# Rounding a float64 weight tile in one ScalarE pass, one float32 product instead of three, and conv taps on TensorE

## The chip, the cores and the metric

The kernel runs on one core of one Trainium2 chip. The metric is the device time of one execution in microseconds, as the median of several runs; lower is better. Beside it stands one execution that the hardware profiler recorded, and all rows below are from that one.

## The reference

Eight batches pass through three blocks. The weights and the conv taps arrive as float64, all else is float32.

```python
# 1. attention between x (8, 8 heads, 512, 64) and state (8, 8, 32, 64)
xread = softmax(x @ state.T / 8) @ state          # 512 rows per head
sread = softmax(state @ x.T / 8) @ x              # 32 rows per head
x = concat(xread, sread)                          # (8, 544, 512)
# 2. gated block: 5 causal conv taps per channel
gate = sigmoid(sum(conv_w[k] * shift(x, 4 - k) for k in range(5)))
x = (gate * (x @ w_val)) @ w_out                  # moe_w_out, 512 x 512
# 3. second block: 3 centred conv taps per channel
h = relu(x @ w_in)                                # 512 x 1024
gate = sigmoid(sum(conv_w2[k] * shift(h, 1 - k) for k in range(3)))
out = (h * gate) @ w_out2                         # moe2_w_out, 1024 x 512
```

## The kernel before

**Two products in one.** Nothing stands between the first block's output matrix (`w_mid` in the kernel) and the second block's input matrix (`w_in`), so the kernel multiplies the two once, at the start, into `wp` (512 by 1024), and every batch uses `wp`. The same holds for the state rows and `w_val`: `a_sw` multiplies the state by `w_val`, and `a_val` multiplies the attention weights by that.

**Halves.** A float32 tile that TensorE is to multiply is split into a high half `hi` (a ScalarE copy to the type fp32r) and a low half `lo = v - hi` (a subtraction, `low`, L137). A product is then three fp32r matmuls, `three` (L161, L162, L163): hi by hi, hi by lo, lo by hi. Products that are made once, such as the scores (L237) and `vals` (L562), are plain float32 matmuls. In `split`, the letters of the table `HOW` say how a low half leaves PSUM: `_` on VectorE, `a` by a ScalarE copy and a GpSimd subtraction, `p` by a matmul with minus the identity and a ScalarE copy. In the rows of `i0`, `i1` and `o`, `l` puts the subtraction of that tile on VectorE and `_` on GpSimd. `c2` names the tiles of batch 0 whose middle tap is multiplied on VectorE.

**Weights.** `fetch` loads a float64 tile of 128 by 512 as raw words of 512 KB. `to_f32` turns it into float32 by integer work on the two 32-bit words of each element: three ScalarE passes (L151, L152, L153), a shift on VectorE (L156) and an integer addition on GpSimd (L158). There are 24 such tiles: four of `w_mid` (`mid`, tokens `m`), eight of `w_in` (`inp`, tokens `i` and, for the loads of the second half, `j`), four of `w_val` (`val`, tokens `v`), eight of `w_out` (`last`, tokens `l`), and one small tile with all conv taps (`taps`, token `k`).

**Order.** Work is written as generators that are started and advanced in an order that stands in five strings. `LOADS` orders the first DMAs, all of them on SyncE's queue. `ORDER` is the set-up: conversion of `w_mid`, the first half of `w_in` and `w_val`, the first half of `wp` (`product0`, tokens `p`, and its way out of PSUM, tokens `q`) and the attention of batch 0. `AHEAD` holds the 16 half steps in which batch b prepares batch b + 1: `L` and `X` load, `t` prepares the state, `x` transposes x, `s` scores, `e`, `r` and `y` read, `w` is `a_sw`, `V` is `a_val`. `AMONG` adds to the steps of batch 0 the second half of `w_in`, the second half of `wp` (`product1`) and `w_out`. `CLOSING` orders the last batch together with the state rows of all batches. The strings set the order of the program; the tile framework then places the instructions on the engines' queues, and each engine works through its own queue in order.

**Steady work.** Per batch and per each of eight blocks of 128 columns, `z_unit` makes 12 matmuls into `z` and the conv and gate (`conv2` L427, `gate2` L432 to L436), and `o_unit` makes 12 matmuls into `o`, two blocks later.

Of the kernel before, what the change touches and what calls it, by code (L numbers as in the profile page):

```python
# [23 lines left out]

LOADS = """
c m0 m1 m2 m3 i2 j2 a i3 i0 v1 i1 v0 v2 j1 j3 j0 v3
"""
ORDER = """  # L30
m1 m0 k m0 v3 i0 m2 t i0 k m0 m2 i1 k m1 m1 i1 m3 i2 m3 i3 i0 m3 v2 m2 m1 i1 v0 i2 m2 m3 x0 x1 x3
t v1 x2 s s i2 v3 e0 e1 s i3 p0 v1 m0 v2 r0 i3 r0 s y0 p1 y0 p2 v0 w r0 p3 r1 y1 q0 w q2 V0 V0 V1
y0 V1 y1 q1 V2 q3 y1 V3 V2 V3 r1
"""

AHEAD = """
L t x0 | | x1 x2 x3 | s | e0 | w X1 e1 | r0 | y0 | X0 r1 | | y1 | X2 V0 | | | | V2 V1 X3 V3
"""

AMONG = """  # L40
i1 i0 | | l0 i2 i3 | p0 | p3 | l1 | p1 l2 | f p2 | | l4 l3 | | l7 | | l6 l5 | |
"""

CLOSING = """
v1 v2 | v0 | v3 O Z E O Z Z | z1 z0 | | | o0 Z Z | Z z2 z4 O O O z3 | o1 O | Z | | O Z | z6 o2 z5
z7 O O | O | o4 | | o67 o5 o3
"""


HOW = {  # L50
    "i0": "l l l _".split(),
    "i1": "l l l l".split(),
    "o": "_ _ l l l l _ _".split(),
    "mT": "_ _ _ a".split(),
    "w0": "a p _ p".split(),
    "w1": "a _ _ p".split(),
    "sw0": "_ a".split(),
    "sw1": "_ a".split(),
    "c2": "_ d _ _ d _ _ _".split(),
}  # L60


# [1 line left out]
def tile_cross_attention_gated_conv_ffn(  # L64
# [74 lines left out]
    def words(raw, dt, k, of=2):  # L139
        return raw.bitcast(dt).rearrange("p (n k) -> p n k", k=of)[:, :, k]  # L140

    def to_f32(dst, raw):

        hi, lo = words(raw, U32, 1).bitcast(F32), words(raw, U32, 0)  # L150
        nc.scalar.activation(dst, hi, AF.Copy, scale=2.0**-112)  # L151
        nc.scalar.activation(lo.bitcast(I32), lo, AF.Copy, scale=2.0**-29)  # L152
        nc.scalar.activation(words(raw, F16, 1, 4), hi, AF.Copy, scale=2.0**-80)  # L153
        yield 0
        d = dst.bitcast(U32)
        nc.vector.tensor_scalar(d, d, 3, None, ALU.logical_shift_left)  # L156
        d = dst.bitcast(I32)
        nc.gpsimd.tensor_tensor(out=d, in0=d, in1=lo.bitcast(I32), op=ALU.add)  # L158

    def three(ps, wh, wl, mh, ml, first, last):  # L160
        nc.tensor.matmul(ps, wh, mh, start=first, stop=False)  # L161
# [102 lines left out]
    def a_score(b):  # L264
        a = A[b]
        sc = [ps_a.tile([P, S], F32, tag="a", name="sc") for _ in range(NG)]
        by_heads(a, sc, lambda pr, u: a["xT"][pr][u, :])
        parts = [score(a, g, sc[g]) for g in range(NG)]
        next(parts[0])
        yield 1  # L270
        next(parts[1])
        next(parts[0])
        yield 1
        next(parts[1])
        next(parts[0], None)
        yield 1
        next(parts[1], None)

    def score(a, g, sc):
        m2 = att.tile([P, 4], F32, tag="m2", name="m2")  # L280
        nc.vector.reduce_max(m2[:, 0:1], sc, axis=AX.X)
        nc.vector.tensor_scalar_mul(m2[:, 1:2], m2[:, 0:1], -SCALE)
        l1 = s_tile("l1", (P, HB, 32))
        nc.vector.transpose(l1.rearrange("p c j -> p (c j)"), sc)
        e2 = s_tile("e2")
        nc.scalar.activation(e2, sc, AF.Exp, scale=SCALE, bias=m2[:, 1:2], accum_out=m2[:, 2:3])
        a["r2"][g], a["e2", g] = m2, e2
        m1 = att.tile([P, HB, 1], F32, tag="m1", name="m1")
        nc.vector.reduce_max(m1, l1, axis=AX.X)
        e1 = s_tile("e1", (P, HB, 32))  # L290
        nc.gpsimd.tensor_tensor(out=e1, in0=l1, in1=m1.to_broadcast([P, HB, 32]), op=ALU.subtract)
        yield
        nc.scalar.activation(e1, e1, AF.Exp, scale=SCALE)
        nc.vector.tensor_scalar_add(m2[:, 2:3], m2[:, 2:3], EPS)
        nc.vector.reciprocal(m2[:, 3:4], m2[:, 2:3])
        r1 = att.tile([P, HB, 1], F32, tag="r1", name="r1")
        nc.vector.reduce_sum(r1, e1, axis=AX.X)
        nc.vector.tensor_scalar_add(r1, r1, EPS)
        nc.vector.reciprocal(r1, r1)
# [57 lines left out]
    def conv1(t, src, ct, taps):  # L357

        for k in taps:
            nc.vector.scalar_tensor_tensor(  # L360
                out=t, in0=src(k), scalar=cw1(ct, k), in1=t, op0=ALU.mult, op1=ALU.add
            )

    def a_xread(b, g):

        a = A[b]
        ps = [ps_a.tile([P, S], F32, tag="a", name="xr") for _ in range(2)]
        for n, (w, m) in enumerate((("nh", "ah"), ("nh", "al"), ("nl", "ah"))):
# [155 lines left out]
    def product_out(ps, hf, c):
        fs = slice(hf * DM, (hf + 1) * DM)
        run(split(wp[:, 0, c, fs], wp[:, 1, c, fs], ps, HOW[f"w{hf}"][c]))

    def val(k):
        yield from to_f32(wv[:, k, :], RAW["v", k])

    def last(f):
        w = f32_tile(True)
        yield from to_f32(w, RAW["o", f])
        yield 1
        W2[f] = w_tile("w2")
        halves(W2[f], w, nc.vector if "l" in HOW["o"][f] else nc.gpsimd)
# [251 lines left out]
```

## Time and profile before

| | |
|---|---|
| median of 3 runs | 592.46 us (591.95 to 592.55) |
| the profiled execution | 591.2 us, of which the span from the first to the last instruction is 589.4 us |
| mean granted TensorE clock | 0.979 of full speed |
| busy over the span | TensorE 94%, VectorE 72%, ScalarE 64%, GpSimd 50% |

In the rows PE is TensorE, PEld its weight loads, DVE VectorE, ACT ScalarE, POOL GpSimd, and SPq SyncE's DMA queue; L153 is line 153 of the kernel. Durations of neighbouring instructions on an engine overlap by about a tenth of a microsecond, and matmuls overlap by more, so the pitch of a sequence is read from start to start.

### The profile page before, as it was taken

What the parts mean: (1) busy time and instruction counts of PE and PEld (TensorE: products, weight loads), DVE (VectorE), ACT (ScalarE), POOL (GpSimd) and SP (SyncE); (2) the same over time, 40 slices, a digit from 0 to 9 for tenths busy, and PEclk for the clock granted to TensorE, in tenths of its full rate; (3) what the DMA queues carried; (4) which work ended last, traced back from release to release, by engine and by line L of the source; (5) the groups of instructions that cost most, each with busy time, mean ns of one, the idle gap of its engine ahead of it and who ended that gap; (6) DMA issues with size and microseconds to landing.
All of it is one profiled execution on the core that took longest, in us unless ns stands there. A gap on an engine that the chain in (4) does not pass through costs nothing.

```text
span 589.4 us, 8728 instructions
## 1 busy us (share of the span) xinstructions
PE 551.1 (94%) x3036; PEld 410.9 (70%) x3036; DVE 423.2 (72%) x691; ACT 375.8 (64%) x699; POOL 295.4 (50%) x374
## 2 busy tenths in 40 slices
PE   0668799989999999999999999999999999999996
PEld 0344566768677867786778677867786778887884
DVE  1465778888599669966996699579957986753452
ACT  8999867785575557555755575556556656654553
POOL 3375669557364536453646354635363625532431
PEclk9957999989999999999999999999999999999999
DMA  6973301630126012701270126010301000100003
GB/s 227 344 256 51 72 9 33 183 71 2 37 60 128 1 47 54 126 0 61 43 121 2 63 48 115 2 63 19 72 0 54 19 1 2 62 10 0 1 1 108
DMA packets 97933, 37.84 MB, mean 64 GB/s; under 512 B 90422, under 2 KB 90466, under 8 KB 97890
## 3 DMA queue, kind: packets, MB, share of 16 engines
q1 hardware_dynamic: 97890, 37.29, 25.1%
q8 instruction: 24, 0.39, 0.3%
q14 instruction: 19, 0.16, 0.1%
HBM read 28.36 MB, written 8.91 MB: 63 GB/s over the span
## 4 chain that ended last, share of the span: by engine, by line
PE 81%; ACT 12%; POOL 2%; DVE 2%; DMA 1%; issue 1%; ACTq 0%; POOLq 0%
PE o L452 10%; PE z L161 10%; PE o L453 10%; PE o L454 9%; PE z L162 9%; PE z L163 9%; PE sw L237 2%; PE val L161 2%; PE val L162 2%; PE val L163 2%; PE xr L371 2%; ACT wir L153 2%; ACT wor L153 1%; PE sr L322 1%; PE sc L237 1%; PE vals L562 1%
## 5 line engine op out<-in xcount | busy, mean ns | idle before, releaser
L427 DVE SCALAR_TENSOR_TENSOR t<-h,cw,t 128x512 f32<-128x512 f32 x128 | 116.5, 914 | 60.6 <-ACT t L425 59.3
L137 POOL TENSOR_TENSOR f<-t,f 128x512 fp32r<-128x512 f32 x64 | 91.2, 1426 | 31.2 <-ACT f L435 30.1
L452 PE MATMUL o<-w,f 128*128 128x512 f32 x256 | 104.5, 410 | 0.2 <-ACT f L435 0.2
L161 PE MATMUL z<-g,wp 128*128 128x512 f32 x256 | 102.8, 402 | 1.0 <-ACT g L397 0.9
L162 PE MATMUL z<-g,wp 128*128 128x512 f32 x256 | 101.4, 396 | 1.1 <-POOL g L137 1.1
L453 PE MATMUL o<-w,f 128*128 128x512 f32 x256 | 101.3, 396 | 0.0
L163 PE MATMUL z<-g,wp 128*128 128x512 f32 x256 | 101.2, 395 | 0.0
L386 DVE SCALAR_TENSOR_TENSOR t<-xr,cw,t 128x510 f32<-128x510 f32 (+3 forms) x128 | 91.0, 740 | 3.8 <-ACT sT L379 2.8
L432 ACT ACTIVATE t<-t 128x512 f32<-128x512 f32 x64 | 40.6, 634 | 78.4 <-DVE t L427 78.4
L454 PE MATMUL o<-w,f 128*128 128x512 f32 x256 | 78.6, 395 | 0.0
L137 POOL TENSOR_TENSOR g<-v,g 128x512 fp32r<-128x512 f32 (+1 forms) x36 | 47.9, 1329 | 39.3 <-ACT g L397 39.2
L452 PEld LDWEIGHTS o<-w,f 128*128 128x128 f32 x256 | 48.4, 189 | 23.7 <-ACT f L435 6.4
L433 DVE SCALAR_TENSOR_TENSOR t<-t,h 128x512 f32<-128x512 f32 x64 | 52.8, 825 | 14.8 <-ACT t L432 14.1
L161 PEld LDWEIGHTS z<-g,wp 128*128 128x128 f32 x256 | 48.1, 188 | 16.9 <-issue 3.0
L435 ACT ACTIVATE f<-t 128x512 fp32r<-128x512 f32 x64 | 40.5, 633 | 28.3 <-DVE t L433 28.3
L162 PEld LDWEIGHTS z<-g,wp 128*128 128x128 f32 x256 | 48.3, 189 | 12.5 <-POOL g L137 1.9
L163 PEld LDWEIGHTS z<-g,wp 128*128 128x128 f32 x256 | 48.2, 188 | 12.4 <-issue 1.2
L442 POOL MEMSET h<- 128x2 f32 x64 | 6.8, 107 | 97.1 <-DVE t L433 96.6
L453 PEld LDWEIGHTS o<-w,f 128*128 128x128 f32 x256 | 48.6, 190 | 9.3
L454 PEld LDWEIGHTS o<-w,f 128*128 128x128 f32 x256 | 47.1, 188 | 10.1 <-issue 0.4
L443 ACT ACTIVATE h<-z 128x512 f32<-128x512 f32 x64 | 38.5, 601 | 22.1 <-PE z L163 21.2
L425 ACT ACTIVATE t<-h,cw 128x512 f32<-128x512 f32 x62 | 45.3, 731 | 1.6 <-POOL h L442 0.4
(164 smaller groups left out, 1017.4 us busy)
## 6 DMA issues: line engine op xcount, KB each, us to landing
xn<-in_x_dram SPq DMA_DIRECT2D x32, 256.0 KB, 4.1
out_dram<-ob SPq DMA_DIRECT2D x26, 256.0 KB, 2.2
y<-in_x_dram SPq DMA_DIRECT2D x96, 64.0 KB, 2.4
wir<-in_moe_w_in_dram SPq DMA_DIRECT2D x8, 512.0 KB, 7.8
wor<-in_moe_w_out_dram SPq DMA_DIRECT2D x8, 512.0 KB, 7.5
wmr<-in_moe_w_out_dram SPq DMA_DIRECT2D x4, 512.0 KB, 4.2
wvr<-in_moe_w_val_dram SPq DMA_DIRECT2D x4, 512.0 KB, 9.1
out_dram<-ob SPq DMA_DIRECT2D x8, 224.0 KB, 2.3
```

The costliest lines, as they stand in the source:

```text
L137: (e or nc.gpsimd).tensor_tensor(out=out, in0=v, in1=hi.bitcast(F32), op=ALU.subtract)
L161: nc.tensor.matmul(ps, wh, mh, start=first, stop=False)
L162: nc.tensor.matmul(ps, wh, ml, start=False, stop=False)
L163: nc.tensor.matmul(ps, wl, mh, start=False, stop=last)
L386: nc.vector.scalar_tensor_tensor(out=t[:, n:], in0=ps[r][:, 0 : S - n], scalar=cw1(ct, k), in1=t[:, n:], op0=ALU.mult, op1=ALU.add,)
L425: nc.scalar.activation(t, h(1), AF.Copy, scale=cw2(f, 1))
L427: nc.vector.scalar_tensor_tensor(out=t, in0=h(k), scalar=cw2(f, k), in1=t, op0=ALU.mult, op1=ALU.add)
L432: nc.scalar.activation(t, t, AF.Tanh, scale=0.5)
L433: nc.vector.scalar_tensor_tensor(out=t, in0=t, scalar=1.0, in1=h, op0=ALU.add, op1=ALU.mult)
L452: nc.tensor.matmul(ps, ft[:, 0, c], W2[f][:, 0], start=first, stop=False)
L453: nc.tensor.matmul(ps, ft[:, 0, c], W2[f][:, 1], start=False, stop=False)
L454: nc.tensor.matmul(ps, ft[:, 1, c], W2[f][:, 0], start=False, stop=last)
```

## The change

`to_f32` takes a letter. Without it, ScalarE makes one pass: the low word times 2^-51, plus 2.0, written as float32, whose bits are 0x40000000 plus the rounded top bits of the low word. VectorE shifts the high word left by 3 straight from the raw tile, GpSimd adds the two as integers, and a new VectorE step puts the sign bit back. With the letter `s` the three old passes stay, and there is no sign step. `HOW` gives `s` to two of the four `w_mid` tiles, three of the eight `w_in` tiles, one of the four `w_val` tiles and one of the eight `w_out` tiles; so 17 of the 24 tiles and the small tile of taps take the new way.

`w_mid` (transposed) and `w_in` are no longer halved: `mid` makes one copy, `inp` converts into the tile that is multiplied, and `product` is one float32 matmul where it was three fp32r ones. Both now live in tiles of the pool `w` in pairs.

The first conv of batch 0 takes, for its first block of channels, four of five taps by float32 matmuls with diagonal matrices (`taps_by_matmul`). In batches 0 and 1 three small operations of `score` per group move from VectorE to ScalarE. `w0`, `sw1` and `c2` get other letters, and all five order strings are new.

```diff
 LOADS = """
-c m0 m1 m2 m3 i2 j2 a i3 i0 v1 i1 v0 v2 j1 j3 j0 v3
+m3 m0 m1 c m2 i2 a i0 i3 i1 j1 v2 v1 v0 j3 j0 v3 j2
 """
 ORDER = """
-m1 m0 k m0 v3 i0 m2 t i0 k m0 m2 i1 k m1 m1 i1 m3 i2 m3 i3 i0 m3 v2 m2 m1 i1 v0 i2 m2 m3 x0 x1 x3
-t v1 x2 s s i2 v3 e0 e1 s i3 p0 v1 m0 v2 r0 i3 r0 s y0 p1 y0 p2 v0 w r0 p3 r1 y1 q0 w q2 V0 V0 V1
-y0 V1 y1 q1 V2 q3 y1 V3 V2 V3 r1
+i0 m1 i1 m1 m0 t m0 m3 i2 k i3 t i0 i0 k m2 k m2 m1 m0 i2 v2 i1 m3 m3 x3 x0 x1 m2 m2 v3 x2 s e0 v3
+m0 v1 s r0 r0 v1 s i1 e1 i2 y0 p0 m3 v0 v0 v2 m1 w i3 w y0 r0 p1 r1 s y0 i3 p2 V0 p3 r1 V1 V0 y1
+V2 V1 q1 y1 q0 V3 y1 V2 V3 q3 q2
 """
 AHEAD = """
-L t x0 | | x1 x2 x3 | s | e0 | w X1 e1 | r0 | y0 | X0 r1 | | y1 | X2 V0 | | | | V2 V1 X3 V3
+x1 | | L x0 x2 t x3 s | | e0 | | w e1 r0 | y0 | r1 | | X2 y1 X0 V0 | V1 | V3 V2 X1 | | X3 |
 """
 AMONG = """
-i1 i0 | | l0 i2 i3 | p0 | p3 | l1 | p1 l2 | f p2 | | l4 l3 | | l7 | | l6 l5 | |
+i2 l0 i3 i1 l1 | | i0 p0 | l2 p3 | | | f p1 | l4 p2 | l3 | | | l7 | l5 | | | l6
 """
 CLOSING = """
-v1 v2 | v0 | v3 O Z E O Z Z | z1 z0 | | | o0 Z Z | Z z2 z4 O O O z3 | o1 O | Z | | O Z | z6 o2 z5
-z7 O O | O | o4 | | o67 o5 o3
+v1 E v2 v3 | | Z v0 | Z Z z1 | O z0 Z | | o0 Z | Z O O O o1 z2 z4 z3 | | Z | O | | O Z o2 z6 z7 O
+| O | z5 o4 O | o67 | O o5 o3
 """
 HOW = {
-    "i0": "l l l _".split(),
-    "i1": "l l l l".split(),
-    "o": "_ _ l l l l _ _".split(),
-    "mT": "_ _ _ a".split(),
-    "w0": "a p _ p".split(),
+    "m": "_ s s _".split(),
+    "i0": "_ _ s _".split(),
+    "i1": "s s _ _".split(),
+    "v": "_ s _ _".split(),
+    "c1": "t _ _ _".split(),
+    "o": "_ _ l l ls _ _ l".split(),
+    "w0": "p _ _ p".split(),
     "w1": "a _ _ p".split(),
     "sw0": "_ a".split(),
-    "sw1": "_ a".split(),
-    "c2": "_ d _ _ d _ _ _".split(),
+    "sw1": "_ _".split(),
+    "c2": "d d d _ _ d _ d".split(),
 }
...
-        hi, lo = words(raw, U32, 1).bitcast(F32), words(raw, U32, 0)
-        nc.scalar.activation(dst, hi, AF.Copy, scale=2.0**-112)
-        nc.scalar.activation(lo.bitcast(I32), lo, AF.Copy, scale=2.0**-29)
-        nc.scalar.activation(words(raw, F16, 1, 4), hi, AF.Copy, scale=2.0**-80)
+        hi, lo = words(raw, U32, 1), words(raw, U32, 0)
+        d = dst.bitcast(U32)
+        if "s" in how:
+            nc.scalar.activation(dst, hi.bitcast(F32), AF.Copy, scale=2.0**-112)
+            nc.scalar.activation(lo.bitcast(I32), lo, AF.Copy, scale=2.0**-29)
+            nc.scalar.activation(words(raw, F16, 1, 4), hi.bitcast(F32), AF.Copy, scale=2.0**-80)
+        else:
+            nc.scalar.activation(lo.bitcast(F32), lo, AF.Copy, scale=2.0**-51, bias=2.0)
         yield 0
-        d = dst.bitcast(U32)
-        nc.vector.tensor_scalar(d, d, 3, None, ALU.logical_shift_left)
-        d = dst.bitcast(I32)
-        nc.gpsimd.tensor_tensor(out=d, in0=d, in1=lo.bitcast(I32), op=ALU.add)
+        nc.vector.tensor_scalar(d, d if "s" in how else hi, 3, None, ALU.logical_shift_left)
+        nc.gpsimd.tensor_tensor(out=dst.bitcast(I32), in0=dst.bitcast(I32), in1=lo.bitcast(I32), op=ALU.add)
+        if "s" not in how:
+            nc.vector.scalar_tensor_tensor(
+                out=d, in0=hi, scalar=0x80000000, in1=d, op0=ALU.bitwise_and, op1=ALU.bitwise_or
+            )
...
+        def scaled(out, x, by, plus):
+            if early:
+                nc.scalar.activation(out, x, AF.Copy, scale=by, bias=plus)
+            else:
+                nc.vector.tensor_scalar(out, x, by, plus, ALU.mult, ALU.add)
...
-        nc.vector.tensor_scalar_mul(m2[:, 1:2], m2[:, 0:1], -SCALE)
+        scaled(m2[:, 1:2], m2[:, 0:1], -SCALE, 0.0)
...
-        nc.vector.tensor_scalar_add(m2[:, 2:3], m2[:, 2:3], EPS)
+        scaled(m2[:, 2:3], m2[:, 2:3], 1.0, EPS)
...
-        nc.vector.tensor_scalar_add(r1, r1, EPS)
+        scaled(r1, r1, 1.0, EPS)
...
+    def taps_by_matmul(t, ct):
+        diag = s_tile("diag", (P, HALO, P))
+        for k in range(HALO):
+            nc.scalar.activation(diag[:, k], ident, AF.Copy, scale=cw1(ct, k))
+        sums = ps_z.tile([P, S], F32, tag="z", name="taps")
+        nc.vector.memset(sums[:, 0:1], 0.0)
+        for k in range(HALO - 1, -1, -1):
+            n = HALO - k
+            nc.tensor.matmul(
+                sums[:, n:], diag[:, k], t[:, 0 : S - n], start=k == HALO - 1, stop=k == 0, skip_group_check=True
+            )
+        nc.vector.scalar_tensor_tensor(
+            out=t, in0=t, scalar=cw1(ct, HALO), in1=sums, op0=ALU.mult, op1=ALU.add
+        )
...
     def mid(c):
...
-        MT[c] = w_tile("mT")
-        run(split(MT[c][:, 0], MT[c][:, 1], ps, HOW["mT"][c], wm))
+        if (c, "both") not in MT:
+            MT[c, "both"] = MT[c ^ 1, "both"] = w_tile("mT")
+        MT[c] = MT[c, "both"][:, c % 2].bitcast(F32)
+        nc.scalar.activation(MT[c], ps, AF.Copy)
     def inp(hf, k):
-        w = f32_tile(True)
-        yield from to_f32(w, RAW["i", hf, k])
-        yield 1
-        WI[hf, k] = g_tile("wi") if hf else f_tile("wi")
-        halves(WI[hf, k], w, nc.vector if "l" in HOW[f"i{hf}"][k] else nc.gpsimd)
+        if (hf, k, "both") not in WI:
+            WI[hf, k, "both"] = WI[hf, k ^ 1, "both"] = w_tile("wi")
+        WI[hf, k] = WI[hf, k, "both"][:, k % 2].bitcast(F32)
+        yield from to_f32(WI[hf, k], RAW["i", hf, k], HOW[f"i{hf}"][k])
     def product(ps, hf, c, ks):
         for k in ks:
-            cs = slice(k * P, (k + 1) * P)
-            wi = WI[hf, k]
-            three(ps, MT[c][:, 0, cs], MT[c][:, 1, cs], wi[:, 0], wi[:, 1], k == 0, k == NCT - 1)
+            nc.tensor.matmul(ps, MT[c][:, k * P : (k + 1) * P], WI[hf, k], start=k == 0, stop=k == NCT - 1)
```

## Rows read from the trace of the kernel before

**Rows 1.** The page: span; busy time, share of the span and instructions of each engine.

```profile
span 589.4 us, 8728 instructions
...
PE 551.1 (94%) x3036; PEld 410.9 (70%) x3036; DVE 423.2 (72%) x691; ACT 375.8 (64%) x699; POOL 295.4 (50%) x374
```

**Rows 2.** Windows: length, busy us (instructions) per engine, clock, DMA share, GB/s.

```profile
0.00:80.20 80.20, 49.34 (x263) 30.46 (x263) 40.43 (x74) 72.52 (x120) 44.13 (x53) 0.87 0.59 176
80.20:150.50 70.30, 68.24 (x359) 50.50 (x356) 59.97 (x94) 50.31 (x92) 47.57 (x48) 0.98 0.27 62
150.50:209.00 58.50, 58.50 (x339) 44.06 (x338) 47.04 (x77) 34.74 (x66) 28.83 (x36) 1.00 0.26 57
...
501.00:589.40 88.40, 83.15 (x403) 66.17 (x402) 43.01 (x72) 43.76 (x91) 31.57 (x59) 1.00 0.09 30
```

**Rows 3.** Windows of 10 us inside the set-up, columns as above.

```profile
30.00:40.00 10.00, 5.33 (x44) 4.04 (x45) 8.55 (x15) 10.00 (x18) 7.22 (x6) 0.50 0.83 320
...
50.00:60.00 10.00, 7.09 (x18) 2.76 (x17) 6.03 (x9) 10.00 (x16) 3.84 (x3) 0.66 0.04 7
```

**Rows 4.** The chain that ended last, at its start: start us, us, what.

```profile
7.16 0.56 ACT wmr L152
7.72 0.54 ACT w L151
8.26 1.23 ACT wmr L153
```

**Rows 5.** Timeline of ACT in the set-up: start us, us, what.

```profile
2.02 0.31 ACT L115 ACTIVATE minus<-ident 128x128 fp32r<-128x128 f32 x1
...
54.31 0.15 ACT L379 ACTIVATE sT<-xr 128x4 f32<-128x4 f32 x1
```

**Rows 6.** Groups of ACT, 0 to 80 us: count, busy us, mean ns.

```profile
L151 ACT ACTIVATE w<-wir 128x512 f32<-128x512 f32 x7 | 4.9, 699 | 0.4 <-POOL w L137 0.4
L498 ACT ACTIVATE wi<-w 128x512 fp32r<-128x512 f32 x7 | 4.3, 653 | 0.0
```

**Rows 7.** Groups of DVE by shape, 0 to 150 us.

```profile
L427 DVE SCALAR_TENSOR_TENSOR t<-h,cw,t 128x512 f32<-128x512 f32 x15 | 16.2, 1082 | 5.2 <-ACT t L425 5.1
...
L137 DVE TENSOR_TENSOR wi<-w,wi 128x512 fp32r<-128x512 f32 x7 | 7.3, 1055 | 1.3 <-ACT wi L498 1.2
L386 DVE SCALAR_TENSOR_TENSOR t<-xr,cw,t 128x511 f32<-128x511 f32 x8 | 5.9, 742 | 1.7 <-ACT sT L379 1.6
...
L137 DVE TENSOR_TENSOR mT<-wmT,mT 128x512 fp32r<-128x512 f32 x3 | 2.1, 692 | 4.4 <-ACT mT L167 4.4
```

**Rows 8.** The page's groups: the same conv step over the whole span.

```profile
L427 DVE SCALAR_TENSOR_TENSOR t<-h,cw,t 128x512 f32<-128x512 f32 x128 | 116.5, 914 | 60.6 <-ACT t L425 59.3
```

**Rows 9.** Groups of all engines: POOL subtractions, 0 to 80 us.

```profile
L137 POOL TENSOR_TENSOR g<-v,g 128x512 fp32r<-128x512 f32 x4 | 5.1, 1278 | 3.0 <-ACT g L397 3.0
```

**Rows 10.** Groups of all engines: POOL subtractions, 80 to 150 us.

```profile
L137 POOL TENSOR_TENSOR f<-t,f 128x512 fp32r<-128x512 f32 x7 | 10.6, 1511 | 0.7 <-ACT f L435 0.7
```

**Rows 11.** The chain that ended last: two stretches of matmuls.

```profile
131.88 0.91 PE o L454 x4
...
498.19 5.18 PE vals L562 x24
```

**Rows 12.** Timeline of PE in the set-up: start us, us, what.

```profile
13.44 0.44 PE L216 MATMUL tp<-ident,s 128*128 128x128 f32 x1 [13.44 <-DMA s<-in_state_dram]
...
38.67 0.63 PE L162 MATMUL wp<-wi,mT 128*128 128x512 f32 x1
39.10 0.63 PE L163 MATMUL wp<-wi,mT 128*128 128x512 f32 x1
```

**Rows 13.** Timeline of PE in batch 0.

```profile
120.35 0.40 PE L163 MATMUL z<-g,wp 128*128 128x512 f32 x1
122.79 0.33 PE L336 MATMUL tps<-ident,srn 128*128 128x128 f32 x1 [2.05 <-DVE srn L330]
```

**Rows 14.** Timeline of SyncE's DMA queue.

```profile
23.26 0.33 SPq L491 DMA_DIRECT2D wvr<-in_moe_w_val_dram  x1
```

More of the change, by code (lines that the diff above doesn't have):

```diff
@@ L140, in words, with to_f32 @@
         return raw.bitcast(dt).rearrange("p (n k) -> p n k", k=of)[:, :, k]
-    def to_f32(dst, raw):
-        hi, lo = words(raw, U32, 1).bitcast(F32), words(raw, U32, 0)
-        nc.scalar.activation(dst, hi, AF.Copy, scale=2.0**-112)
-        nc.scalar.activation(lo.bitcast(I32), lo, AF.Copy, scale=2.0**-29)
-        nc.scalar.activation(words(raw, F16, 1, 4), hi, AF.Copy, scale=2.0**-80)
-        yield 0
-        d = dst.bitcast(U32)
-        nc.vector.tensor_scalar(d, d, 3, None, ALU.logical_shift_left)
-        d = dst.bitcast(I32)
-        nc.gpsimd.tensor_tensor(out=d, in0=d, in1=lo.bitcast(I32), op=ALU.add)
+    def to_f32(dst, raw, how="_"):
+        hi, lo = words(raw, U32, 1), words(raw, U32, 0)
[6 more added lines that the diff above has]
+            nc.scalar.activation(lo.bitcast(F32), lo, AF.Copy, scale=2.0**-51, bias=2.0)
+        yield 0
+        nc.vector.tensor_scalar(d, d if "s" in how else hi, 3, None, ALU.logical_shift_left)
[4 more added lines that the diff above has]
+            )
     def three(ps, wh, wl, mh, ml, first, last):
@@ L267, in a_score @@
         by_heads(a, sc, lambda pr, u: a["xT"][pr][u, :])
-        parts = [score(a, g, sc[g]) for g in range(NG)]
+        parts = [score(a, g, sc[g], b < EARLY) for g in range(NG)]
         next(parts[0])
@@ L277, in a_score, with score @@
         next(parts[1], None)
-    def score(a, g, sc):
+    def score(a, g, sc, early):
+        def scaled(out, x, by, plus):
[3 more added lines that the diff above has]
+                nc.vector.tensor_scalar(out, x, by, plus, ALU.mult, ALU.add)
         m2 = att.tile([P, 4], F32, tag="m2", name="m2")
         nc.vector.reduce_max(m2[:, 0:1], sc, axis=AX.X)
-        nc.vector.tensor_scalar_mul(m2[:, 1:2], m2[:, 0:1], -SCALE)
+        scaled(m2[:, 1:2], m2[:, 0:1], -SCALE, 0.0)
         l1 = s_tile("l1", (P, HB, 32))
@@ L377, in a_xread @@
             t = t_tile("t1")
-            nc.scalar.activation(t, ps[r], AF.Copy, scale=cw1(ct, HALO))
+            if b == 0 and "t" in HOW["c1"][ct]:
+                nc.scalar.activation(t, ps[r], AF.Copy)
+            else:
+                nc.scalar.activation(t, ps[r], AF.Copy, scale=cw1(ct, HALO))
             nc.scalar.activation(sT[:, ct, b, 0:HALO], ps[r][:, S - HALO : S], AF.Copy)
@@ L383, in a_xread @@
             yield 1
+            if b == 0 and "t" in HOW["c1"][ct]:
+                taps_by_matmul(t, ct)
             for k in range(HALO - 1, -1, -1):
+                if b == 0 and "t" in HOW["c1"][ct]:
+                    break
                 n = HALO - k
@@ L502, in mid @@
         wm = f32_tile()
-        yield from to_f32(wm, RAW["m", c])
+        yield from to_f32(wm, RAW["m", c], HOW["m"][c])
         yield 1
@@ L528, in val @@
     def val(k):
-        yield from to_f32(wv[:, k, :], RAW["v", k])
+        yield from to_f32(wv[:, k, :], RAW["v", k], HOW["v"][k])
     def last(f):
         w = f32_tile(True)
-        yield from to_f32(w, RAW["o", f])
+        yield from to_f32(w, RAW["o", f], HOW["o"][f])
         yield 1
```

## The prediction

> **What bounds the kernel now.** I read the page's busy shares first [rows 1]. TensorE at 94% looks like the bound, but a share is a mean over stages, so I cut the span where batches begin [rows 2]. The reader is to see three regimes. From 150.5 us on, a batch takes 58.4 us with TensorE busy in all of it at full clock, while VectorE is busy 80% and ScalarE 59%: only fewer matmuls could shorten these batches, and the change takes none away there. In the first 80.2 us, the set-up, TensorE is busy 49.3 us at a mean clock of 0.87 and ScalarE 72.5 us. Inside it ScalarE has no idle time in 30 to 40 or 50 to 60 us, and TensorE, fed in pieces, falls to a mean clock of 0.50 and 0.66 there [rows 3]. So ScalarE sets the length of the set-up. Batch 0, from 80.2 to 150.5 us, takes 70.3 us, 12 more than a steady batch, with VectorE at 85%. The last 88.4 us are again TensorE's.
>
> The chain of waits shows what ScalarE does in the set-up: it goes from conversion pass to conversion pass, at 0.56 (L152), 0.54 (L151) and 1.23 us (L153) [rows 4].
>
> **ScalarE in the set-up.** In the set-up 20 of the 24 tiles go through L153; by the new letters 14 of them lose it: 14 x 1.23 = 17.2 us. L151 goes too, for the 11 of those tiles whose L151 lies in the set-up: 11 x 0.55 = 6.1 us. The third pass, L152, stays as the new pass with a bias, same shape and same operands: 0. The taps' tile is a quarter as wide: 0.5 us. The halves of `w_in` go, seven copies at a pitch of 0.56 [rows 6]: 3.9 us; two ScalarE copies of `split` at about 0.5 go: 1.0. That is 28.7 us off. Added: four diagonals at 0.3, priced by the 128x128 copy of 0.31, and six tiny operations at 0.2, priced by the 128x4 copy of 0.15 [rows 5]: 2.4. Net -26.3 us; ScalarE's load falls from 72.5 to 46.2 us. With the idle time that it has now (80.2 - 72.5 = 7.7) the set-up could not be under 53.9 us.
>
> **VectorE and GpSimd there.** The new sign step is not in the trace. It is a two-input step with both inputs in SBUF, like L427; L386 has one input in PSUM. L427 takes 0.91 us over the span and 1.08 in the first 150 us, L386 0.74 [rows 7, 8]. So a sign step costs 0.74 to 1.08; I take 0.91. The shift now reads every second word; I leave its price as it is, and 0.3 more each, 4 us, as the other end. In the set-up: 14 x 0.91 = 12.7 in; out go three `w_mid` subtractions at 0.69, four of `w_in` at 1.06, three conv taps at 0.74 and small operations of 1.2, and one subtraction of `w0` comes in at 0.7 [rows 7]. VectorE goes from 40.4 to 44.1 us. GpSimd loses three subtractions at 1.28 [rows 9] and keeps its additions: 44.1 to 40.3.
>
> The Trainium skill, GPSIMD Engine Reference, section 1 (Specifications), says that GpSimd shares its SBUF interfaces with VectorE and contends with VectorE instructions that have two SBUF inputs. The trace agrees: 1.08 against 0.74 us. By that rule the sum would move from the forecast towards the second rival below.
>
> **TensorE there.** A float32 matmul of 256 columns is two records of 0.216 us [rows 11]; of 512 columns, 0.863. Three fp32r matmuls are 3 x 0.2275 = 0.683 [rows 11]. The 16 products of a half of `wp` thus cost 16 x 0.18 = 2.9 us more, and the four taps 4 x 0.863 = 3.4 us. In the set-up TensorE's busy time becomes 49.3 + 6.3 = 55.6 us. It can't start before the first state rows land, at 13.44 [rows 12]: 69.0 us if it were as slow as now, and less as products no longer run at half clock, where an fp32r matmul takes 0.43 instead of 0.23 [rows 12].
>
> **The loads.** `LOADS` changes only the order on SyncE's queue. The last weight of the set-up is issued at 23.26 us [rows 14], and by 50 to 60 us the DMA share is 0.04 [rows 3]; what uses it comes 20 us later even in a shorter set-up. Priced at 0; without that cover a late tile costs its conversion chain, some 3 us.
>
> **Length of the new set-up.** The ends are 53.9 (ScalarE, as well packed as now) and 69.0 (TensorE, as badly clocked as now). Three engines now carry 44 to 56 us each, and each has to wait for the others in the chain pass, shift, add, sign, matmul, copy, where one engine with a full queue could run at 90%. So I take a value above the middle: 64 us, a gain of 16.2.
>
> **Batch 0.** The second half of `wp` lies in a stretch where TensorE is nearly full [rows 2]: +2.9 on the path. VectorE gets seven sign steps (6.4), three more middle taps (2.2) and one subtraction (0.7), and loses three `w_in` subtractions (3.2) and small operations (1.5): +4.6 on 60.0 us, 88% of a 73 us stretch. This is where the sign step adds a wait: it stands in VectorE's queue until GpSimd's addition of 1.28 us is done, and behind it wait L427 and L433, for which ScalarE, GpSimd and at last TensorE wait. The price is between 0 (other VectorE work is placed between) and 4.6; I take 2.0. ScalarE's relief here (the passes of `w_out`) shortens nothing by itself, since it is busy 50 of 70 us.
>
> **Steady batches and the end.** `AHEAD` moves transposes, reads and `V` among half steps, `CLOSING` the state blocks. With TensorE busy all the time [rows 2], an order changes nothing as long as no operand comes late: 0. If that cover fails, the third rival gives the price.
>
> **Sum.** Against the profiled execution: 591.2 - 16.2 + 2.9 + 2.0 = 579.9 us. The median of the runs shown is 1.3 above that execution: 581.2 us.
>
> **The rivals.** (1) ScalarE stays the only clock of the set-up, and batch 0 hides its VectorE work: 53.9 us of set-up, 591.2 - 26.3 + 2.9 + 1.3 = 569.1. For it: ScalarE's 90% now. Against it: three other engines above 40 us in 54, and TensorE's late start. Chance 0.12.
>
> (2) Sign steps and GpSimd's additions hold each other up. GpSimd's subtractions take 1.28 us in the set-up [rows 9] and 1.51 in batch 0 [rows 10], where VectorE works more, so each of 21 sign steps until 150 us costs another 0.17 on VectorE and 0.23 on GpSimd: 8.4 us, if all lies on the path. 581.2 + 8.4 = 589.6. For it: the stretched rows; against it: in the set-up neither engine is full. Chance 0.15.
>
> (3) Slower: the new `AHEAD` leaves a hole in each batch. The place is the first half step, where `x1` now needs its y load of a late half step of the batch before, and the reads one step on. The price is that of the hole in batch 0 now: TensorE waits from 120.35 + 0.23 to 122.79, 2.2 us [rows 13], and if it then runs eight matmuls at half clock [rows 12], that is 8 x 0.2 = 1.6 more. 3.8 us in each of six batches is 22.8: 604.0. It decides from 1.9 us per batch (11.3 / 6). Against it: steady batches have slack on all other engines. Chance 0.07.
>
> **How the numbers follow.** Forecast 0.62, with a range of its own: set-up 57 to 69 and batch 0 at 0 to 4.6 give 572 to 589. Rivals 0.12, 0.15, 0.07; 0.04 for gains that are lost elsewhere, without a change that shows. The range 570 to 590 takes in the forecast, most of (2) and part of (1). About 0.2%, 1.2 us, is what a measurement of this kernel can tell from no change. Faster: 0.62 + 0.12 + 0.13 of (2) = 0.87; within: 0.05; slower: (3) and a rest, 0.08.
>
> **What would show it.** In the new profile: 128x512 passes of L153's kind seven instead of 24; ScalarE's busy time until the first dense `z` near 46 us, and that point near 64 us; product matmuls at 0.86 us per 512 columns; sign steps between 0.74 and 1.08; batch 0 some 75 us long with VectorE near 88%; steady batches at 58.4 us. The prediction is wrong if the set-up still ends past 75 us, whatever engine then fills it, or if a steady batch departs by more than 0.5 us.

## The result and the profile after

The changed kernel takes 586.86 us (median of 4 runs, 585.02 to 587.41), the kernel before, run beside it, 592.50 (591.95 to 592.77): a ratio of 0.990, with a 95% interval of 0.9877 to 0.9924. That is faster, by 5.6 us where 11.3 were predicted. The profiled execution is the shortest of the four, 585.02 us with a span of 583.2, so the two profiles differ by 6.2 us.

The page of the changed kernel, its first lines:

```profile
span 583.2 us, 8633 instructions
...
PE 554.3 (95%) x3012; PEld 404.9 (69%) x3012; DVE 424.6 (73%) x690; ACT 344.0 (59%) x665; POOL 288.2 (49%) x370
```

Against [rows 1] only ScalarE has changed much, 375.8 to 344.0 us. The windows by stage below are the counterpart of [rows 2]. The set-up ends, as before, where the last three matmuls of the first `z` start; batch 0 then lasts to the first `z` of batch 1 (150.8 us before; [rows 2] cut it at 150.5).

```profile
0.00:73.40 73.40, 51.34 (x247) 27.86 (x247) 45.26 (x75) 50.65 (x97) 44.85 (x52) 0.95 0.64 191
73.40:146.60 73.20, 69.97 (x349) 46.70 (x350) 60.71 (x91) 40.60 (x82) 42.75 (x44) 1.00 0.27 61
146.60:205.10 58.50, 58.50 (x338) 44.45 (x337) 44.78 (x76) 34.99 (x66) 26.41 (x36) 1.00 0.27 56
438.60:583.20 144.60, 141.01 (x739) 110.29 (x737) 89.78 (x145) 78.64 (x158) 57.27 (x94) 1.00 0.08 26
```

| stage | predicted | measured |
|---|---|---|
| set-up | 80.2 to 64, -16.2 | 80.2 to 73.4, -6.8 |
| batch 0 | +4.9 | 70.6 to 73.2, +2.6 |
| batches 1 to 5 | 0 | 291.9 to 292.0, +0.1 |
| from the first `z` of batch 6 to the end | 0 | 146.7 to 144.6, -2.1 |

ScalarE's load in the set-up fell from 72.5 to 50.7 us; it is busy in 69% of the new set-up and no longer sets its length. Four stretches of the set-up show where TensorE now stands idle:

```profile
0.00:25.00 25.00, 6.74 (x28) 5.66 (x29) 9.92 (x16) 14.82 (x24) 12.99 (x27) 1.00 0.85 276
25.00:43.00 18.00, 18.00 (x60) 7.63 (x59) 12.54 (x24) 16.41 (x34) 10.18 (x9) 1.00 0.85 293
43.00:62.00 19.00, 16.35 (x119) 7.33 (x118) 14.08 (x23) 12.55 (x29) 15.25 (x13) 0.91 0.48 86
62.00:73.40 11.40, 10.25 (x44) 7.24 (x44) 8.72 (x14) 6.87 (x14) 6.42 (x6) 0.85 0.09 15
```

In the first 25 us TensorE is busy 6.74 us, with the DMA engines at a mean share of 0.85. ScalarE's and TensorE's timelines say why:

```profile
21.00 0.67 ACT L163 ACTIVATE wir<-wir 128x512 f32<-128x512 uint32 x1 [5.96 <-DMA wir<-in_moe_w_in_dram]
21.57 1.55 ACT L552 ACTIVATE mT<-wmT 128x512 f32<-128x512 f32 x3
```

```profile
22.20 2.82 PE L270 MATMUL tpx<-ident,xn 128*128 128x128 f32 x12 [5.86 <-ACT mT L552]
24.81 1.91 PE L562 MATMUL wp<-wi,mT 128*128 128x512 f32 x2
```

ScalarE stands 5.96 us in front of a `w_in` tile that lands at 21.0; the copies `mT` are queued behind that pass, TensorE waits 5.86 us for them, and the first product comes at 24.81. Before, the first product came at 36.8 us, after a copy of `w_in` by ScalarE. So the products start 12 us earlier, and a load now holds their start, through ScalarE's queue, where ScalarE's work did. The scores, with which batch 0's attention begins, start later than before: at 28.8 and 36.8 us instead of 23.0 and 24.5.

### The profile page after: what moved, and what is told of

Read it like the earlier page. It is cut to its first block, busy times and chain, and to the rows that moved or that the text cites. A ratio compares the mean times of both kernels' runs of the same rounds, so it can differ in the third digit from the quotient of the medians.

```text
span 583.2 us, 8633 instructions
## 1 busy us (share of the span) xinstructions
PE 554.3 (95%) x3012; PEld 404.9 (69%) x3012; DVE 424.6 (73%) x690; ACT 344.0 (59%) x665; POOL 288.2 (49%) x370
## 4 chain that ended last, share of the span: by engine, by line
PE 81%; DMA 7%; DVE 5%; SPq 2%; ACT 2%; POOL 1%; issue 1%; DVEq 0%; ACTq 0%
PE o L493 10%; PE o L495 10%; PE z L173 10%; PE o L494 10%; PE z L174 9%; PE z L175 9%; DMA wir<-in_moe_w_in_dram 4%; PE val L173 3%; PE val L174 3%; PE val L175 3%; DMA wor<-in_moe_w_out_dram 2%; PE xr L405 2%; PE sw L249 2%; DVE t L468 1%; PE sr L340 1%; PE sc L249 1%
## 5 line engine op out<-in xcount | busy, mean ns | idle before, releaser
L468 DVE SCALAR_TENSOR_TENSOR t<-h,cw,t 128x512 f32<-128x512 f32 x128 | 112.4, 882 | 56.2 <-ACT t L466 55.1
L140 POOL TENSOR_TENSOR f<-t,f 128x512 fp32r<-128x512 f32 x64 | 88.3, 1380 | 32.2 <-ACT f L476 32.2
L427 DVE SCALAR_TENSOR_TENSOR t<-xr,cw,t 128x511 f32<-128x511 f32 (+3 forms) x124 | 88.8, 740 | 5.9 <-ACT sT L416 5.0
L493 PEld LDWEIGHTS o<-w,f 128*128 128x128 f32 x256 | 48.1, 188 | 23.3 <-ACT f L476 5.9
L484 ACT ACTIVATE h<-z 128x512 f32<-128x512 f32 x64 | 38.3, 598 | 21.2 <-PE z L175 20.4
L466 ACT ACTIVATE t<-h,cw 128x512 f32<-128x512 f32 x59 | 43.1, 730 | 1.1
```

What stands on the lines that cost most here:

```text
L140: (e or nc.gpsimd).tensor_tensor(out=out, in0=v, in1=hi.bitcast(F32), op=ALU.subtract)
L427: nc.vector.scalar_tensor_tensor(out=t[:, n:], in0=ps[r][:, 0 : S - n], scalar=cw1(ct, k), in1=t[:, n:], op0=ALU.mult, op1=ALU.add,)
L466: nc.scalar.activation(t, h(1), AF.Copy, scale=cw2(f, 1))
L468: nc.vector.scalar_tensor_tensor(out=t, in0=h(k), scalar=cw2(f, k), in1=t, op0=ALU.mult, op1=ALU.add)
L493: nc.tensor.matmul(ps, ft[:, 0, c], W2[f][:, 0], start=first, stop=False)
```

## The experiments

Times are medians; a span is that of the profiled execution. "Slower" and "faster" are against the changed kernel, each taken by its distance from the kernel before that ran beside it (592.5 to 593.1 us).

One thing holds for all runs but the eighth. The strings and the edits set the order of the program, and the framework places the steps on the queues anew for each kernel. In runs 1 to 7, 9, 11 and 12 VectorE's queue has steps of the set-up in another order than in the changed kernel, steps that the edit doesn't name among them; run 10 differs in this way from the kernel before. So each of these runs measures its edit together with a new placement, and none of them separates the two.

**1. The first `w_in` tiles ahead of state and `x`** (token `a` loads both).

```diff
-m3 m0 m1 c m2 i2 a i0 i3 i1 j1 v2 v1 v0 j3 j0 v3 j2
+m3 m0 m1 c m2 i2 i0 i3 i1 a j1 v2 v1 v0 j3 j0 v3 j2
```

> The changed kernel with the four first-half w_in tiles loaded ahead of x. Theory A (the set-up is now set by what has landed: no product can start before 24.8 us, ScalarE stands 6 us in its queue on a w_in tile, with copies of mT behind it): the first product starts some 4 us earlier and the time falls to about 583. Theory B (TensorE's float32 products and taps fill the set-up): its work is the same, 587. Theory C (sign steps and GpSimd's additions hold each other up): the same, 587.

593.59 us, ratio to the kernel before 1.0014 (1.0 to 1.0028): 6.5 us slower (0.9 above the kernel before, which is 5.6 above the changed one). The products start at 23.3 us, but the state's first matmul at 15.87 instead of 10.97, and the scores of both groups at 33.6 and 45.5 instead of 28.8 and 36.8; batch 1 starts at 155.4 instead of 146.6. No theory gave a slower kernel. What is put ahead pushes something else back, so this run can't say what the earlier landing alone is worth; run 5 takes the wait away in another way.

**2. Half of the first products left out.** The kernel leaves out two of four terms in the first half of `wp`, 6.9 us of TensorE.

```diff
         for c in range(NCT):
-            product(pp[c], 0, c, [k])
+            if k in (0, NCT - 1):
+                product(pp[c], 0, c, [k])
```

> The changed kernel without the products of k = 1 and 2 in the first half of wp: 8 of 16 float32 products, 6.9 us of TensorE, are left out, so the output is not the reference's. Theory B: the whole 6.9 us comes off, 580. Theory A: only what stands ahead of the second scores counts, about 3.5 us, 583, since the chain of the attention behind it stays. Theory C: the same, 587.

591.26 us, ratio 0.9976 (0.9962 to 0.9989): 4.2 us slower with less work. The products end at 35.6 us instead of 43.1, yet the second read of x, `xr`, starts at 65.7 instead of 59.6: additions and sign steps of the second half of `w_in` now stand ahead of the softmax steps in GpSimd's and VectorE's queues. VectorE in the changed kernel, where the second group's `m<-l` comes first, and then in this run:

```profile
40.77 0.67 DVE L307 TENSOR_REDUCE m<-l 128x16 f32<-128x512 f32 x1
...
43.23 1.52 DVE L168 SCALAR_TENSOR_TENSOR wi<-wir,wi 128x512 uint32<-128x512 uint32 x1 [0.52 <-POOL wi L166]
```

```profile
40.38 0.67 DVE L168 SCALAR_TENSOR_TENSOR wi<-wir,wi 128x512 uint32<-128x512 uint32 x1
...
41.58 0.67 DVE L307 TENSOR_REDUCE m<-l 128x16 f32<-128x512 f32 x1
```

The set-up ends at 79.2 us, and no theory gave a slower kernel. Less work on TensorE came with a longer set-up; what it would be worth with the queues as they were is not shown.

**3. All taps on VectorE again.**

```diff
-    "c1": "t _ _ _".split(),
+    "c1": "_ _ _ _".split(),
```

> The changed kernel with all conv taps of batch 0 on VectorE again. Theory B: 3.5 us of TensorE come off, 583.5. Theory A: 586 to 588, three VectorE steps in place of the matmuls. Theory C: VectorE gets 2.2 us more, 589.

588.60 us, ratio 0.9926 (0.9903 to 0.9949). By the medians the taps by matmul are worth 1.5 us, by the spans 0.9 (584.1), although they add 3.6 us to TensorE. The interval overlaps that of the changed kernel (0.9877 to 0.9924), so a gain is likely but not clear of noise. Theory B's 583.5 is out.

**4. Halves and three fp32r products again**, new rounding kept.

```diff
-        MT[c] = MT[c, "both"][:, c % 2].bitcast(F32)
-        nc.scalar.activation(MT[c], ps, AF.Copy)
+        MT[c] = w_tile("mT")
+        run(split(MT[c][:, 0], MT[c][:, 1], ps, "_ _ _ a".split()[c], wm))
...
-            nc.tensor.matmul(ps, MT[c][:, k * P : (k + 1) * P], WI[hf, k], start=k == 0, stop=k == NCT - 1)
+            three(ps, MT[c][:, 0, cs], MT[c][:, 1, cs], wi[:, 0], wi[:, 1], k == 0, k == NCT - 1)
```

> The changed kernel with w_mid and w_in in halves and three fp32r matmuls again. Theory B: 2.9 us of TensorE come off in each half of wp, 581. Theory A: ScalarE's eight copies and the eleven subtractions come back into the chain before the products, 588 to 592. Theory C: VectorE and GpSimd get 9 us more, 592 or more.

592.51 us, ratio 0.9996 (0.9979 to 1.0013), 5.4 us slower: in these orders, without the float32 product, the gain is gone. Theory B's 581 is out; A and C both reach here. Windows of this run, set-up, batch 0 and batch 1:

```profile
0.00:71.10 71.10, 48.87 (x274) 31.27 (x274) 48.29 (x79) 52.65 (x102) 45.50 (x52) 0.95 0.66 197
71.10:152.10 81.00, 71.70 (x363) 49.75 (x357) 65.70 (x96) 43.06 (x85) 45.67 (x46) 0.92 0.25 55
152.10:214.00 61.90, 60.46 (x337) 45.92 (x334) 49.01 (x79) 34.88 (x67) 29.88 (x37) 1.00 0.24 53
```

The set-up is not longer; batch 0 is, by 7.8 us with VectorE at 65.7 instead of 60.7, and batch 1 by 3.4.

**5. The waiting `w_in` pass behind the `mT` copies** on ScalarE's queue; its tokens follow those of `m0` in `ORDER`. The lines below, and those of runs 6, 7 and 11, are shortened to what the edit does.

```diff
+        with tc.issue_after(copy_of_mT_0):      # queue order only
             next(gen)                           # the ScalarE pass of w_in tile 0
```

> Computes everything. The one ScalarE pass of the first w_in tile is put behind the copies of the transposed w_mid tiles on ScalarE's queue, where the new kernel has it in front of them and waits 5.9 us (15.0 to 21.0) for that tile to land. Theory D (the set-up ends with batch 0's attention chain, and its small steps stand in the in-order queues behind conversion steps): the transposes of x start near 17 to 19 instead of 22.2 us, the scores near 25 instead of 28.8, the first dense z near 70 instead of 73.4, total 2 to 4 us under the new kernel, 583 to 585. Theory E (the engines' added-up loads set the length, so a wait at the start is made good later): within 1 us of the new kernel, 586 to 588.

586.99 us, ratio 0.9896 (0.9874 to 0.9917): no change. Yet the edit did what it was for. The transposes of x start at 17.0 us instead of 22.2, the scores at 23.3 and 29.0 instead of 28.8 and 36.8, the first high half `ah` of the attention weights at 38.3 instead of 44.1. What was won is lost one queue further on. VectorE, then TensorE:

```profile
43.72 1.52 DVE L168 SCALAR_TENSOR_TENSOR wi<-wir,wi 128x512 uint32<-128x512 uint32 x1 [1.03 <-POOL wi L166]
...
46.96 0.33 DVE L348 TENSOR_SCALAR srn<-sr,m 128x128 f32<-128x128 f32 x1
```

```profile
47.34 0.79 PE L405 MATMUL xr<-ah,nh 64*128 64x512 f32 x1 [1.50 <-DVE srn L348]
```

A sign step, which itself waits 1.03 us for GpSimd, stands ahead of `srn` (the state's read, scaled), with three other steps between them, and TensorE's next step comes at 47.34 us, as it did in the changed kernel. The set-up ends at 73.3 us.

**6. Conversions that batch 0 needs later put later**: three second-half `w_in` tiles and two `w_out` tiles behind the last attention weights of batch 0, on all three engines. **7. Both edits together.**

```diff
+        with tc.issue_after(a1), tc.issue_after(ah), tc.issue_after(al):   # of group 1
             next(gen)                           # each conversion step of those tiles
```

> Computes everything. The conversions of three second-half w_in tiles and two w_out tiles, which batch 0 needs some 20 us later, are put behind batch 0's last attention weights (transpose on VectorE, high half on ScalarE, low half on GpSimd). Theory D: the second group's softmax steps come 2 to 4 us earlier, the first dense z near 70 to 71 instead of 73.4; part of it is lost in batch 0, where the conversions now lie; total 584 to 587. Theory E (loads): the same work lies in the same 146.6 us before batch 1, total 586 to 588, and the set-up's gain comes back as a longer batch 0.

> Computes everything: the edits of the two runs before together. Theory D: the gains add, the first dense z near 67 to 68, total 581 to 585. Theory E: 586 to 588, as for each alone.

593.87 us, ratio 1.0013 (0.9998 to 1.0028), and 594.54 us, ratio 1.0039 (1.0023 to 1.0054): 6.5 and 7.2 us slower, which neither theory gave. In run 7 the second `ah` comes at 43.2 us instead of 54.0, and still `sw`, the product of the state, starts no earlier (49.4 in the changed kernel): conversion passes, most of them held back by the edit, and two copies of `wp` now fill ScalarE from 43.7 to 49 us, ahead of a copy that TensorE waits for. ScalarE, then TensorE:

```profile
49.10 0.57 ACT L333 ACTIVATE e2T<-tpe 128x512 f32<-128x512 f32 x1
```

```profile
49.73 1.93 PE L249 MATMUL sw<-wv,stT 64*32 64x512 f32 x8 [0.80 <-ACT e2T L333]
```

The set-up ends at 77.2 and 75.1 us, and batch 0 takes 76.5 and 79.8 us instead of 73.2, with VectorE at 62.2 and 66.3 us instead of 60.7.

**8. `CLOSING` of the kernel before**, all else new.

```diff
-v1 E v2 v3 | | Z v0 | Z Z z1 | O z0 Z | | o0 Z | Z O O O o1 z2 z4 z3 | | Z | O | | O Z o2 z6 z7 O
-| O | z5 o4 O | o67 | O o5 o3
+v1 v2 | v0 | v3 O Z E O Z Z | z1 z0 | | | o0 Z Z | Z z2 z4 O O O z3 | o1 O | Z | | O Z | z6 o2 z5
+z7 O O | O | o4 | | o67 o5 o3
```

> Computes everything. The new kernel with the CLOSING order of the kernel before, all else new. If the 2.1 us that the end became shorter (146.7 to 144.6 us from the first z of the sixth batch) come from the order of the closing steps: 2 us slower than the new kernel, 588.5 to 589.5, with the stretch from that z to the end at 146.5 to 147. If they come from something else (less work held over from the batches): the same as the new kernel, 586 to 587.5.

588.40 us, ratio 0.9931 (0.9908 to 0.9954), 1.1 us slower, with an interval that overlaps that of the changed kernel. The profile decides: from the first `z` of batch 6 to the end it takes 146.6 us instead of 144.6.

```profile
438.50:585.10 146.60, 141.38 (x739) 110.18 (x737) 89.00 (x145) 79.29 (x158) 58.38 (x94) 1.00 0.08 26
```

The same stretch is 146.6 to 146.7 us in both other kernels with the old `CLOSING` (the kernel before and run 10) and 144.6 to 144.7 in the changed kernel and in all other runs. So the 2 us at the end of the profile are the order's. Until there this kernel's queues are those of the changed kernel, so it also shows what two executions of the same instructions do: this one has its set-up done at 71.3 us instead of 73.4, and both start batch 1 at 146.6. A difference of 2 us in the end of the set-up is thus no finding by itself.

**9. The old three passes for every tile** in the changed kernel. **10. The new rounding alone** in the kernel before.

```diff
-    "m": "_ s s _".split(),
-    "i0": "_ _ s _".split(),
+    "m": "s s s s".split(),
+    "i0": "s s s s".split(),
...
```

Run 9 has `s` for `i1`, `v`, `o` and the tile of taps too; run 10 puts the new `to_f32` with its letters into the kernel before.

> Computes everything. The new kernel with the three old ScalarE passes and no sign step for every tile (letter s everywhere, the tile of taps too); float32 product, taps by matmul, orders as in the new kernel. Theory P (the prediction's step: ScalarE's relief shortens the set-up): ScalarE gets back 14 x 1.8 = 25 us in the set-up, the first dense z goes from 73.4 back to 80 or later, total 6 us or more above the new kernel, 593 or more. Theory D (the set-up's end is a chain whose steps wait in turn in all queues; the passes are only one of them): it comes 2 to 5 us later, total 589 to 592.

> Computes everything. The kernel before with the new way of rounding alone (one pass, shift from the raw tile, addition, sign step for the 17 tiles with the new letters); halves, three fp32r products, taps on VectorE and all orders as in the kernel before. Theory P: the set-up shortens by most of what it did in the new kernel, first dense z near 73 to 75 instead of 80.2, total 586 to 589. Theory D: VectorE and GpSimd, which still make the halves, now carry the sign steps too; the set-up ends 0 to 4 us earlier and batch 0 becomes longer by as much, total 590 to 594.

605.33 us, ratio 1.0204 (1.0185 to 1.0223), and 601.18 us, ratio 1.0134 (1.0118 to 1.0150). In the changed kernel, with its orders, the rounding is worth 17.9 us; by itself, with the halves and orders of before, it costs 8.1. Run 9 bears out theory P's "593 or more"; run 10 is above what either theory gave. The orders of run 9 were made for the new passes, and how much of the 17.9 us is theirs the run doesn't split. Run 9, the set-up; run 10, set-up, batch 0 and batch 1:

```profile
0.00:91.70 91.70, 53.63 (x258) 27.49 (x258) 34.99 (x62) 73.09 (x126) 43.13 (x53) 0.89 0.51 153
```

```profile
0.00:75.30 75.30, 48.91 (x267) 31.37 (x267) 51.86 (x85) 52.79 (x94) 46.34 (x53) 0.86 0.63 187
75.30:153.30 78.00, 69.71 (x359) 50.93 (x354) 69.65 (x102) 45.31 (x84) 49.87 (x48) 0.96 0.25 56
153.30:215.70 62.40, 61.76 (x338) 43.86 (x337) 44.04 (x75) 33.87 (x65) 28.94 (x36) 1.00 0.25 53
```

Alone, it shortens the set-up by 4.9 us and lengthens batch 0 by 7.4 and batch 1 by 4.1: VectorE carries the sign steps and all subtractions of the halves too, 69.65 us in batch 0 instead of the 59.97 of [rows 2].

**11. The tap matmuls behind the state product** on TensorE's queue.

```diff
+        with tc.issue_after(last_sw_matmul):
             nc.tensor.matmul(sums[:, n:], diag[:, k], t[:, 0 : S - n], ...)
```

> Computes everything. The tap matmuls of batch 0 (3.7 us) are put behind the second half of the state-by-w_val matmuls on TensorE's queue, where the new kernel has them ahead of it. If the stretch from 49 us on is paced by TensorE's queue order (the second half of that product, its halves and then the values wait for the taps): the values start 1 to 3 us earlier than 57.1 us, the first dense z near 71 to 72.5, total 1 to 2 us under the new kernel. If it is paced by VectorE's conv steps or by PSUM buffers that they free: within 0.7 us of the new kernel.

586.08 us, ratio 0.9881 (0.9861 to 0.9901), 1.3 us faster, with an interval that overlaps that of the changed kernel; the spans say the opposite (584.4 against 583.2). After a wait of 1.22 us for a conv step of VectorE the values start at 56.3 us instead of 57.1, and then wait 1.54 us for a copy of VectorE; the set-up ends at 73.9. Neither theory is shown.

**12. Runs 5 and 11 together, and the second read of x ahead of the values.**

```diff
-... w y0 r0 p1 r1 s y0 i3 p2 V0 p3 r1 V1 V0 y1 V2 V1 q1 y1 q0 V3 y1 V2 V3 q3 q2
+... w y0 r0 p1 s y0 y1 i3 p2 V0 p3 r1 r1 V1 y1 V0 V2 y1 V1 q1 q0 V3 V2 V3 q3 q2
```

> Computes everything. The first run with the w_in pass behind the copies, together with the tap matmuls behind the state product, and the read of x for the second group moved ahead of the values of the first two blocks and of the second state read in the order of the set-up. If the last link of the set-up is second read of x, conv steps, v, g of the last two blocks on VectorE (theory D): that read starts near 55 to 57 instead of 59.6 us, the last g 2 to 3 us earlier, the first dense z near 70.5 to 71.5, total 1.5 to 3 us under the new kernel, 584 to 585.5. If VectorE's added work from 45 us on sets the end, whatever its order: first dense z within 0.8 of 73.4, total 586 to 588.

590.18 us, ratio 0.9956 (0.9939 to 0.9972), 2.9 us slower, neither of the two. The read starts at 55.2 us as expected, VectorE has its conv steps done by 65.5, but TensorE meanwhile runs for much of the time at the lower of its two clock levels:

```profile
61.24 1.08 PE L341 MATMUL sr<-xn,e2T 128*32 128x64 f32 x32 [0.86 <-DVE v L438]
...
64.28 0.63 PE L173 MATMUL val<-ah,swh 128*128 128x512 f32 x1
64.70 0.63 PE L174 MATMUL val<-al,swh 128*128 128x512 f32 x1
```

The pitch is 0.43 us for matmuls that take 0.23 at full clock (granted clock 0.71 from 62 to 74 us, where the changed kernel has 0.86), the third `v` comes at 71.4 us instead of 68.3, and the set-up ends at 76.3. How much of this is the clock's and how much the new order's is not shown.

## Why the prediction was right, and where it was wrong

**The direction and the steps that held.** Faster, inside the range, with half of the predicted gain. 2.1 of the 6.2 us between the profiles come from the end, which was priced at 0; that the total came no lower than half is in part luck. ScalarE's load in the set-up fell from 72.5 to 50.7 us (46.2 predicted), and runs 9 and 10 bear out that this shortens the set-up. Products run at 0.43 us a record, 0.86 per 512 columns. The 17 sign steps take 1.05 us in the mean, within 0.74 to 1.08, where 0.91 was taken. The shift from the raw tile is no dearer than the old one: 0.42 us over seven `w_out` tiles and 0.81 over five of `w_in`, beside 0.64 over the 20 old shifts of `w` in the kernel before. A steady batch is 58.4 to 58.5 us.

```profile
L168 DVE SCALAR_TENSOR_TENSOR w<-wor,w 128x512 uint32<-128x512 uint32 x7 | 8.5, 1217 | 0.5 <-POOL w L166 0.5
L168 DVE SCALAR_TENSOR_TENSOR wi<-wir,wi 128x512 uint32<-128x512 uint32 x5 | 4.7, 931 | 1.7 <-POOL wi L166 1.7
```

**The step that failed: "Length of the new set-up", with "The loads. Priced at 0".** The set-up was taken at 64 us between ends of 53.9 and 69.0; it is 73.4 (71.3 in run 8's execution), above even the upper end. That end was 13.4 us before TensorE's first work plus 55.6 us of work, one after the other, with no wait once TensorE has begun. TensorE is busy 51.3 us in the end, less than that, but idle 22.1: 11.0 before its first work, 5.9 for the copies `mT` and 5.2 in smaller pieces. The waits after its start, 11.1 us, are the term that was left at nothing. Of the other engines' work VectorE's came out at 45.3 us (44.1 predicted) and GpSimd's at 44.9 (40.3).

The loads were priced by the last tile, which indeed nobody waits for; it is a first one that TensorE stood for. With ScalarE relieved, the landing of a `w_in` tile at 21.0 us became the thing that the copies, and so TensorE, wait for. That is shown by the rows. But this wait does not set the length: run 5 takes it away and ends the set-up at 73.3 us. Its rows show one place where the time goes, a step of the attention that is ready and stands in an engine's queue behind a conversion step of another tile, and run 7 shows a second one. That the whole set-up from 43 us on is such a chain over four queues is argued from these two. Eight runs (1, 2, 3, 5, 6, 7, 11, 12) each pushed on one suspect or two, some moved a stage of the chain by up to 11 us, and none started batch 1 before 146.6 us. What the shortest set-up of this work would be with an order made for it stays open.

The Trainium skill, Perfetto Trace Analysis, section Per-instruction lifecycle, says that ScalarE, VectorE and GpSimd work through their queues strictly in order. The traces agree: in run 5 the `srn` step comes at 46.96 us, behind a sign step that waits 1.03 us, though TensorE had written its operand `sr` by 41.6 us.

**"Batch 0" and TensorE's float32 product.** The product was a cost of 2.9 us on the path and VectorE's 4.6 us a cost of 2.0. Together batch 0 grew by 2.6 instead of 4.9. VectorE's work there rose by some 0.7 us, from 60.0 to 60.7, not by 4.6: the sum counted 14 sign steps in the set-up and seven in batch 0, 21, where 17 of the 24 tiles take the new way; the trace has 12 and five. (With 17, rival (2) would have been 588.0.) And the two terms belong together: in run 4 the product is worth 5.4 us, and run 10 shows that the rounding without it loses more in batches 0 and 1 than it wins in the set-up. The likely reason is that the product takes the subtractions of the halves off VectorE: with VectorE at 65.7 and 69.7 us of work (runs 4 and 10), batch 0 takes 81.0 and 78.0 us; at 60.7, 73.2. As the longer batch 0 goes with the smaller of those two amounts, VectorE's work is not the only cause.

The predicted mechanism is in the trace. In batch 0 a copy that TensorE needs stands behind sign steps; VectorE's timeline, and TensorE's after it:

```profile
116.85 1.78 DVE L168 SCALAR_TENSOR_TENSOR w<-wor,w 128x512 uint32<-128x512 uint32 x1
118.56 1.76 DVE L468 SCALAR_TENSOR_TENSOR t<-h,cw,t 128x512 f32<-128x512 f32 x1
120.24 0.68 DVE L168 SCALAR_TENSOR_TENSOR w<-wor,w 128x512 uint32<-128x512 uint32 x1
120.85 0.45 DVE L357 COPY sT<-tps 64x64 f32<-64x64 f32 x2
```

```profile
121.44 0.47 PE L173 MATMUL val<-ah,swh 128*128 128x512 f32 x1 [3.14 <-DVE sT L357]
```

TensorE stands for 3.14 us. The kernel before had a hole of about 2 us at the step just ahead of this one in the same chain, where the transposition `tps` waited for VectorE's `srn` [rows 13].

**"Steady batches and the end".** Steady batches as predicted. The end was priced at 0 on the ground that an order changes nothing while TensorE is busy; but it was busy only 83.15 of the last 88.4 us [rows 2], and run 8 shows that the new `CLOSING` takes 2 us off the end.

**The rivals.** ScalarE as the only engine that sets the set-up's length (569.1) is out: it is busy in 69% of the set-up. The hole per batch is out: 58.4 to 58.5 us. Sign steps against GpSimd (589.6) came nearest by the number. Contention is there, as the last section shows; how much of the missing 5.7 us it costs, no run tells.

## What to carry to other kernels

When the engine that sets the length of a stage is relieved, list what arrives first and not only what arrives last: here the landing of an early tile was the next wait, and behind it stood others, so that taking it away gained nothing. A length between two bounds from busy times is no estimate for a stage that is a chain over several in-order queues; there, follow the chain step by step and count what is queued ahead of each. Count the added steps tile by tile, so that none is in two stages. Price edits that load and unload the same engine together: the rounding alone lost 8 us, and the change without the float32 product gained nothing. And after an edit compare the queues, not only the time: if the framework has placed other steps anew, the run has changed two things.

## What the runs showed of the hardware

The same VectorE step takes 0.68 or 1.78 us. GpSimd's timeline beside the four VectorE rows above:

```profile
115.00 4.77 POOL L166 TENSOR_TENSOR w<-w,wor 128x512 int32<-128x512 int32 x3 [0.43 <-POOL hl L485]
```

While its three additions run, to 119.77 us, the sign step takes 1.78 and the conv step 1.76; the sign step that starts after them takes 0.68. Contention had been read as 1.08 against 0.74 from means, which mix both cases. One by one, the additions end at 116.38, 118.09 and 119.77 us. The VectorE steps that start under them, at 115.83 (a conv step of 1.10 us), 116.85 and 118.56, each end 0.54 or 0.55 us after that: each waits for the addition's end and then takes its own time. The other way round, a subtraction with two SBUF inputs at 122.54 us takes 0.68, while GpSimd's own, which starts 0.05 us later, takes 1.79 instead of some 1.28. So in these rows the two engines take turns, and the one that started first goes ahead; no run here tests that by moving one step alone.

Time won can be given back by TensorE's clock, which runs at one of two levels. In run 8 the same instructions come 1.6 us earlier to the hole of batch 0 (`val` at 119.85 instead of 121.44 us); after it matmuls in run 8 come at a pitch of 0.43 us for 3 us, then at 0.23 again (granted clock 0.83 from 115 to 125 us), in the changed kernel's profile at 0.23 throughout (1.00), and both reach the next `o` at 127.05 and 127.07. Run 5 shows 0.83 there too. Why one execution keeps the clock after a hole of 3.1 us and another with 3.2 doesn't, the traces here don't show.
